# The state's part of the outputs as 64x64 matmuls, with r laid out by token half

## The chip, the cores and the metric

The kernel runs on one core of a Trainium2 chip. The metric is the device time of one execution in microseconds; the time before is the median of three runs. The engines are named as in the profile: PE (TensorE), ACT (ScalarE), DVE (VectorE), POOL (GpSimd), SP (the queue that issues most transfers).

## The reference

A linear attention with a decaying state (4 batches, 8 heads, 768 tokens, 48 values per head), followed by a dense two-layer network with SiLU on the 3072 tokens of 384 values:

```python
for t in range(S):
    cur = np.einsum('bhd,bhe->bhde', u[None] * kt, vt)
    y[:, :, t] = np.einsum('bhd,bhde->bhe', rt, state + cur)
    state = w[None, :, :, None] * state + np.einsum('bhd,bhe->bhde', kt, vt)
...
h = x @ w_in                       # 384 -> 2048
g = h * (1.0 / (1.0 + np.exp(-h)))
out = g @ w_out                    # 2048 -> 384
```

Inputs and outputs are float32.

## The kernel before

The tokens are cut into six chunks of 128, and a unit is one chunk of one batch: unit i is chunk i // 4 of batch i % 4, 24 units in all. Units are worked in pairs (i, i+1; the code calls the member e = 0 or 1). From unit 4 on a chunk is cut again into two halves of 64 tokens (x = 0 or 1). For the first half of a chunk the state that counts is the one carried from the chunk before; for the second half it is the state after the first half.

Heads lie in pairs: after `turn`, head 2p+j (j = 0 or 1) of r and k has its 48 values in partitions 64j to 64j+47 (rows 48 to 63 are a pad), with p and the token along the free dimension. `decay_one` multiplies by powers of w and gives `rT` and `kT` in float32; `cast_r` (L271) makes `rT16`, the 16-bit copy of `rT`, 112 partitions x 4 head pairs x 128 tokens.

The state stands in `st` in float32, 112 partitions: head j of each pair in rows 64j to 64j+47, 48 columns for each head pair p and member e. Two kinds of 16-bit copies of it feed the matmuls: `carry` (s0h in the profile, three buffers, the carried state) and `inner` (s1h, two buffers, the state after the first half). Before the change both are in a block form: for each member and head pair a matrix of 112 rows and 96 columns with head 0 in the upper left block, head 1 in the lower right one, and zeros elsewhere, set once at the start by five memsets (L143). `spread_state` (L330) writes the two blocks by two copies of 48 partitions x 384 elements. `first_state` does that on DVE for the first chunk, `state_first` on ACT for `inner`, `next_state` on POOL for `carry`.

The outputs of a pair, `outputs_halves` (L415), come in two groups of matmuls into two PSUM tiles `yp[e]`. The state's part (L424): for each head pair, member and half one matmul with 112 rows of `rT16` as weights (64 tokens) and the 96 columns of the block form, 16 matmuls. The attention's part (L433): for each head, member and half one matmul of 64 rows, 64 tokens and 48 columns, 32 matmuls. The half x and the member e set the rows of `yp` through `rows(e, x)`, so that the four matmuls of one head use four different quarters of the array.

PSUM has two tiles `att` for the transposes and the products of r and k, and four buffers under the tag `moe`, given out in turn to whatever asks: the network's first layer `hps`, its second layer `ops`, the sums `sp` and the outputs `yp`.

The order is written out by hand and each engine keeps it (`manual_schedule`). A list of words (`order`) places the steps of units 0 to 7 between pieces of the network (L and G for one tile of the first layer and its SiLU, H for both); in it `r16` is `cast_r` on ACT, `v16` the cast of v, `sd` the decay of the carried state, `sn` is `next_state`, `Z` the outputs and `z` their eviction. Then a loop runs over the pairs 6, 8, ..., 22. A round does: the sums of k and v (`sums`, L374), the products, both states, four network pieces (`fill(4)`), the outputs, the transposes of the next pair, the eviction on DVE, its transposed transfer, 4 pieces, the casts of v, then for each unit of the next pair two pieces and `cast_r` on DVE (L273), and 4 pieces more. A piece is one first-layer tile with its SiLU on ACT (L477, L485) or a quarter of a second-layer tile (L498), whose last quarter is followed by its copy `osb` (L504). When the pair is 2 or 3 of its chunk, sixteen first-layer and sixteen second-layer pieces are added to the list after the outputs.

Of the kernel before, what the change touches and what calls it, by code (L numbers as in the profile page):

```python
# [9 lines left out]
F16 = mybir.dt.float16  # L10
# [5 lines left out]
def kernel(  # L16
# [11 lines left out]
    nc = tc.nc  # L28

    B, H, S, D = r.shape  # L30
    C = 128
    NCH = S // C
    HD = H * D
    NP = H // 2
    PW = 2 * D
    PR = 64 + D
# [5 lines left out]
    HC = C // 2  # L42

    cst = ctx.enter_context(tc.tile_pool(name="cst", bufs=1))
    big = ctx.enter_context(tc.tile_pool(name="big", bufs=1))
    wrk = ctx.enter_context(tc.tile_pool(name="wrk", bufs=2))
# [3 lines left out]
    def unit(i):  # L50
        return divmod(i, B)
# [14 lines left out]
    st = [big.tile([PR, 2, NP, D], FP, name=f"st{b}") for b in range(B // 2)]  # L66
# [3 lines left out]
    def ld(i, dst, src, eng=nc.sync):  # L70
        sc, b = unit(i)
        eng.dma_start(
            out=dst[i % NIN][:, :, 0:D],
            in_=src[b, :, sc * C:sc * C + C, :].rearrange("h t d -> t h d"))
# [54 lines left out]
    for y in range(2):  # L129
# [5 lines left out]
        out=maskM, in_=maskM, compare_op=ALU.is_ge, fill=0.0,  # L135
# [1 line left out]
    ident16 = cst.tile([128, 128], F16)  # L137
    nc.gpsimd.tensor_copy(out=ident16, in_=ident)
    maskH = cst.tile([128, HC], FP)
    carry = [big.tile([PR, 2, NP, PW], F16, name=f"s0h{n}") for n in range(3)]  # L140
    inner = [big.tile([PR, 2, NP, PW], F16, name=f"s1h{n}") for n in range(2)]
    for t in carry + inner:
        nc.vector.memset(t, 0.0)  # L143
    for i in range(NIN):
        nc.gpsimd.memset(kc[i][:, :, D:64], 0.0)

# [62 lines left out]
    def L(i):  # L209
        return live.setdefault(i, {})  # L210
# [57 lines left out]
        decay_one(i, 0)  # L268
        decay_one(i, 1)

    def cast_r(i, copy=nc.vector.tensor_copy):  # L271
        L(i)["rT16"] = wrk.tile([PR, NP, C], F16, name="rT16", bufs=4)
        copy(out=L(i)["rT16"], in_=L(i)["rT"])  # L273

    def product_pair(i):
        a = [next_att().rearrange("p j (g c) -> p j g c", g=NP) for _ in range(2)]
# [50 lines left out]
    def carried_in(i):  # L327
        return carry[i // 2 % 3]

    def spread_state(copy, dst, src):  # L330
        for p0, c0 in ((0, 0), (64, D)):
            copy(out=dst[p0:p0 + D, :, :, c0:c0 + D], in_=src[p0:p0 + D])  # L332

    def first_state(i):
        _, b = unit(i)
        spread_state(nc.vector.tensor_copy, carried_in(i + B), L(i)["sps"])
        nc.vector.tensor_copy(out=st[b // 2], in_=L(i)["sps"])

    def rows(e, x):
        return HC * (x ^ e)  # L340

    def product_halves(i):
        a = next_att().rearrange("p j (e g c) -> p j e g c", e=2, g=NP)
        L(i)["a2"] = a
        for p in range(NP):
            for e in range(2):
                rT, kT = L(i + e)["rT"], L(i + e)["kT"]
                for x in range(2):
                    o0 = HC * x
                    for j, r0 in ((0, 0), (1, 64)):  # L350
                        nc.tensor.matmul(a[o0:o0 + HC, j, e, p, :],  # L351
                                         kT[r0:r0 + D, p, HC * x:HC * x + HC],
                                         rT[r0:r0 + D, p, HC * x:HC * x + HC],
                                         start=True, stop=True)
# [8 lines left out]
    def sums(i):  # L363
        sc, b = unit(i)
        xs = range(2 if sc < NCH - 1 else 1)
        L(i)["sp"] = [ps.tile([128, 512], FP, name="sp", tag="moe", bufs=4) for _ in xs]
        for p in range(NP):
            for e in range(2):
                for x in xs:
                    rows = slice(HC * x, HC * x + HC)  # L370
                    for j in range(2):
                        h = 2 * p + j
                        c0 = (e * NP + p) * D
                        nc.tensor.matmul(L(i)["sp"][x][64 * j:64 * j + 64, c0:c0 + D],  # L374
                                         kc[(i + e) % NIN][rows, h, :],
                                         L(i + e)["v16"][rows, h, :],
                                         start=True, stop=True)

    def flat(t):
        return t.rearrange("p e g n -> p (e g n)")  # L380

    def w_half():
        return wHT.unsqueeze(1).unsqueeze(3).broadcast_to([PR, 2, NP, D])

    def state_first(i):
        s1 = L(i)["s1"] = wrk.tile([PR, 2, NP, D], FP, name="s1")
        nc.vector.tensor_tensor(out=flat(s1), in0=L(i)["sp"][0][0:PR, 0:HD],  # L387
                                in1=flat(L(i)["sdec"]), op=ALU.add)
        spread_state(nc.scalar.copy, inner[i // 2 % 2], s1)

    def state_second(i):
        sc, b = unit(i)
        if sc == NCH - 1:
            return
        sd = wrk.tile([PR, 2, NP, D], FP, name="sd")
        nc.vector.tensor_tensor(out=sd, in0=L(i)["s1"], in1=w_half(), op=ALU.mult)
        nc.vector.tensor_tensor(out=flat(st[b // 2]), in0=L(i)["sp"][1][0:PR, 0:HD],
                                in1=flat(sd), op=ALU.add)

    def decayed_state(i):  # L400
        _, b = unit(i)
        L(i)["sdec"] = wrk.tile([PR, 2, NP, D], FP, name="sdec", bufs=3)
        nc.gpsimd.tensor_tensor(out=L(i)["sdec"], in0=st[b // 2], in1=w_half(), op=ALU.mult)

    def next_state(i):
        sc, b = unit(i)
        if sc == NCH - 1:
            return
        spread_state(nc.gpsimd.tensor_copy, carried_in(i + B), st[b // 2])
        decayed_state(i + B)  # L410

    def outputs_halves(i):
        yp = L(i)["y2"] = [ps.tile([128, 512], FP, name="yp", tag="moe", bufs=4)
                           for _ in range(2)]

        def place(e, x, c0, n):
            y0 = rows(e, x)
            return yp[e][y0:y0 + HC, c0:c0 + n]

        for p in range(NP):  # L420
            for e in range(2):
                for x in (e, 1 - e):
                    s = inner[i // 2 % 2] if x else carried_in(i)
                    nc.tensor.matmul(place(e, x, PW * p, PW),  # L424
                                     L(i + e)["rT16"][:, p, HC * x:HC * x + HC], s[:, e, p, :],
                                     start=(p == 0), stop=False, skip_group_check=True)
        for p in range(NP):
            for j in range(2):
                h = 2 * p + j
                for e in range(2):  # L430
                    for x in range(2):
                        r = HC * x
                        nc.tensor.matmul(place(e, x, D * h, D), L(i)["am2"][r:r + HC, j, e, p, :],  # L433
                                         L(i + e)["v16"][r:r + HC, h, :],
                                         start=False, stop=True, skip_group_check=True)

    def evict_halves(i):
        yp = L(i)["y2"]
# [117 lines left out]
    def piece(word, f):  # L556
# [12 lines left out]
        "vu": bonus_v,  # L569
        "Y": outputs_y, "y16": evict_first, "yT": turn_y, "xT": copy_x,  # L570
        "S": first_sums, "st": first_state, "ku": bonus_ku, "ru": bonus_rku, "rd": bonus_sum,
        "r16": lambda i: cast_r(i, nc.scalar.copy), "sd": decayed_state, "i_q": ld_win, "i_o": ld_wout,
        "Q": sums, "P": product_halves, "m": masked_halves, "s1_": state_first,
        "s2_": state_second, "sn": next_state, "Z": outputs_halves, "z": evict_halves,
        "lr": lambda i: ld(i, rin, r), "lk": lambda i: ld(i, kin, k), "lv": lambda i: ld(i, vin, v),
    }
    order = """
# [6 lines left out]
        L4.10 G4.10 T5 kT5 rT5 L4.11 G4.11 vu4 ru5 i_o0 v165 Q4 P4 s1_4 m4 rd5 s2_4 r165  # L584
        L4.12 G4.12 vu5 i_o1 L4.13 G4.13 Z4 z4 L4.14 G4.14 L4.15 G4.15 yT4 xT4
        yT5 xT5 T6 kT6 rT6 kc6 ku6 ru6 i_o2 H0 H1 v166 r166 H2 H3 T7 kT7 rT7 kc7 ku7 i_o3 v167
        r167 H4 ru7 rd6 sd6 vu6 sn4
    """
    for word in order.split():
        if "*" in word:  # L590
            n, word = word.split("*")
# [18 lines left out]
    for i in range(B + 2, NU, 2):  # L610
        sc, b = unit(i)
        nxt = range(i + 2, min(i + 4, NU))
        sums(i)
        product_halves(i)
        state_first(i)
        state_second(i)
        masked_halves(i)
        if i == B + 2:
            bonus_sum(i + 1)
            bonus_v(i + 1)  # L620
        for n in nxt:
            bonus_products(n)
            decayed_k(n)
        if i > B + 2 or sc < NCH - 1:
            next_state(i)
        fill(4)
        outputs_halves(i)
        for n in nxt:
            turn(n)
        evict_halves(i)  # L630
        turn_y_dma(i)
        turn_y_dma(i + 1)
        if b:
            fillers.extend((first(sc) if sc > 1 else rest_first(sc)) + second(sc))
        for n in nxt:
            decay(n)
        load(i + B)
        load(i + 1 + B)
        fill(4)
        for n in nxt:  # L640
            bonus_sum(n)
            cast_v(n)
            bonus_v(n)
        for n in nxt:
            fill(2)
            cast_r(n)
        fill(4)
    fill(len(fillers))

# [29 lines left out]
```

## Time and profile before

| what | value |
|---|---|
| median of 3 runs | 192.3 us (191.97 to 192.69) |
| the profiled execution's own time | 192.8 us |
| its span | 191.0 us |
| mean granted clock | 0.997 |
| PE busy | 180.1 us |
| ACT busy | 99.0 us |
| DVE busy | 114.7 us |
| POOL busy | 118.6 us |

The span is the time from the first to the last instruction of the profiled execution. A busy time is the union of an engine's instructions; matmuls are pipelined, so their rows overlap. In the timeline a row is the start in us, the time that the merged instructions took, engine, line, operation, output and inputs, shape, count, and in brackets the idle time before and what ended it. In the groups the columns are the count, the busy us, the mean ns of one, and the idle us before them with their causes. In the windows the columns are the stretch and its length, then the busy us and instructions of PE, PEld (weight loads), DVE, ACT and POOL, the granted clock, the share of the DMA engines and GB/s. The slices cut the span in 40 parts, with a digit for tenths busy.

### The profile page before, as it was taken

The page shows a single profiled execution, that of the slowest core. Times are in us where ns is not written, and L with a number is a line of the kernel's source. Part 1 is how long each engine was busy: PE and PEld are TensorE (multiplying, and loading weights), DVE is VectorE, ACT ScalarE, POOL GpSimd, SP SyncE. Part 2 cuts the span into 40 slices and gives each one's busy share as a digit, 9 for nine tenths or more (in the row PEclk, how much of TensorE's full clock was granted, in tenths as well). Part 3 has the DMA queues.
Part 4 walks back from the last instruction along what each step waited for, and adds up shares of the span by engine and source line. Part 5 has one row for each costly group of instructions (what it writes and reads, how often), then busy time and mean ns, then how long its engine had stood idle before and what let it go on. Part 6 is the DMA issues. An engine that isn't in the chain of part 4 may idle for free. (4 is left out here: it accounts for less than half of the span.)

```text
span 191.0 us, 6511 instructions
## 1 busy us (share of the span) xinstructions
PE 180.1 (94%) x2786; PEld 113.1 (59%) x2786; DVE 114.7 (60%) x189; ACT 99.0 (52%) x193; POOL 118.6 (62%) x151
## 2 busy tenths in 40 slices
PE   7798898998999999999999999999999999999993
PEld 2454783677666786655656655656646566444562
DVE  7578876845884794695686775766853944200120
ACT  5394477576433293158573178563267643289200
POOL 6499989699899977849649649749659130000000
PEclk9999999999999999999999999999999999999998
DMA  5999979999959469269177269177386202310022
GB/s 95 209 191 189 207 149 184 155 218 222 148 113 195 148 134 200 65 129 223 26 147 165 65 138 209 32 146 165 84 177 163 41 4 82 85 42 0 6 79 84
DMA packets 90272, 24.42 MB, mean 128 GB/s; under 512 B 83329, under 2 KB 90242, under 8 KB 90242
## 3 DMA queue, kind: packets, MB, share of 16 engines
q1 hardware_dynamic: 84992, 20.39, 49.1%
q0 software_dynamic: 3712, 3.15, 10.8%
q10 hardware_dynamic: 1538, 0.46, 1.1%
q8 instruction: 22, 0.36, 0.8%
q14 instruction: 8, 0.07, 0.1%
HBM read 20.65 MB, written 4.72 MB: 133 GB/s over the span
## 5 line engine op out<-in xcount | busy, mean ns | idle before, releaser
L477 PE MATMUL hps<-xT,win 128*128 128x512 f16 (+1 forms) x360 | 66.4, 337 | 1.0 <-DMA xT<-y 0.5
L485 ACT ACTIVATE gT<-hps 128x512 f16<-128x512 f32 x96 | 55.8, 597 | 17.4 <-PE hps L477 14.2
L498 PE MATMUL ops<-wout,gT 128*128 128x384 f16 x368 | 62.5, 326 | 0.0
L477 PEld LDWEIGHTS <-win 128*128 128x128 f16 x360 | 33.8, 98 | 26.8 <-issue 1.6
L498 PEld LDWEIGHTS <-gT 128*128 128x128 f16 x368 | 35.2, 98 | 23.4
L236 POOL TENSOR_TENSOR vu<-vin,rku 128x384 f32<-128x384 f32 x24 | 21.1, 892 | 21.0 <-DVE rku L231 21.0
L218 POOL TENSOR_TENSOR ku<-kin,u_bc 128x384 f32<-128x384 f32 x24 | 24.4, 1018 | 11.1 <-DMA kin<-in_k_dram 7.5
L504 ACT COPY osb<-ops 128x384 f32<-128x384 f32 x20 | 9.6, 479 | 41.7 <-PE ops L498 31.1
L305 DVE TENSOR_TENSOR y<-yp,vu 64x384 f16<-64x384 f32 (+1 forms) x34 | 18.9, 555 | 13.7 <-PE yp L433 5.0
L222 POOL TENSOR_TENSOR rku_f<-rin,ku 128x384 f32<-128x384 f32 x24 | 24.3, 1012 | 1.7
L226 POOL TENSOR_TENSOR kc<-kin,lamH 128x384 f16<-128x384 f32 x20 | 20.7, 1038 | 0.0
L259 DVE TENSOR_TENSOR kT<-att,lamK 112x512 f32<-112x512 f32 x24 | 16.4, 683 | 4.8 <-PE att L251 4.8
L387 DVE TENSOR_TENSOR s<-sp,sdec 112x384 f32<-112x384 f32 x10 | 5.6, 558 | 22.0 <-PE sp L374 20.7
L259 DVE TENSOR_TENSOR rT<-att,lamR 112x512 f32<-112x512 f32 x24 | 16.5, 686 | 2.5 <-PE att L251 1.1
L332 ACT CAST s1h<-s 48x384 f16<-48x384 f32 x20 | 10.2, 511 | 9.6 <-DVE s L387 9.5
L242 ACT CAST v<-vin 128x384 f16<-128x384 f32 x24 | 11.5, 511 | 5.4 <-DMA vin<-in_v_dram 5.2
L506 DVE COPY osb<-ops 128x384 f32<-128x384 f32 x3 | 1.7, 558 | 20.6 <-issue 16.5
L273 DVE CAST rT<-rT 112x512 f16<-112x512 f32 x16 | 13.9, 906 | 0.0
L231 DVE TENSOR_REDUCE rku<-rku_f 128x8 f32<-128x384 f32 x24 | 12.5, 544 | 1.4 <-POOL rku_f L222 1.4
L358 DVE TENSOR_TENSOR am<-att,maskH 128x1024 f16<-128x1024 f32 x10 | 12.2, 1218 | 1.2 <-PE att L351 1.2
L351 PE MATMUL att<-rT,kT 48*64 48x64 f32 x640 | 11.6, 220 | 0.0
L251 PE MATMUL att<-ident,kin 64*112 64x64 f32 x192 | 9.4, 217 | 1.5 <-DMA kin<-in_k_dram 1.5
(74 smaller groups left out, 167.1 us busy)
## 6 DMA issues: line engine op xcount, KB each, us to landing
rin<-in_r_dram SPq DMA_DIRECT2D x24, 192.0 KB, 3.7
vin<-in_v_dram SPq DMA_DIRECT2D x24, 192.0 KB, 4.3
kin<-in_k_dram SPq DMA_DIRECT2D x23, 192.0 KB, 4.5
out_dram<-osb SPq DMA_DIRECT2D x23, 192.0 KB, 2.7
win<-in_moe_w_in_dram POOLq DMA_DIRECT2D x4, 384.0 KB, 6.5
wout<-in_moe_w_out_dram POOLq DMA_DIRECT2D x4, 384.0 KB, 6.2
xT<-y SPq DMA_TRANSPOSE x18, 2.3
kin<-in_k_dram ACTq DMA_DIRECT2D x1, 192.0 KB, 3.7
```

Of the source, the lines that this page charges most:

```text
L218: nc.gpsimd.tensor_tensor(out=L(i)["ku"], in0=kin[i % NIN][:, :, 0:D], in1=u_bc, op=ALU.mult)
L222: nc.gpsimd.tensor_tensor(out=L(i)["rku_f"], in0=rin[i % NIN][:, :, 0:D], in1=L(i)["ku"], op=ALU.mult)
L226: nc.gpsimd.tensor_tensor(out=kc[i % NIN][:, :, 0:D], in0=kin[i % NIN][:, :, 0:D], in1=lamH if unit(i)[0] else lamC, op=ALU.mult)
L231: nc.vector.tensor_reduce(out=L(i)["rku"], in_=L(i)["rku_f"], axis=mybir.AxisListType.X, op=ALU.add)
L236: nc.gpsimd.tensor_tensor(out=L(i)["vu"], in0=vin[i % NIN], in1=L(i)["rku"].unsqueeze(2).broadcast_to([128, H, D]), op=ALU.mult)
L259: nc.vector.tensor_tensor(out=L(i)[key].rearrange("p g (y t) -> p y g t", y=2), in0=L(i)["t"][0:PR, :, x], in1=lam, op=ALU.mult)
L273: copy(out=L(i)["rT16"], in_=L(i)["rT"])
L305: nc.vector.tensor_tensor(out=y16[a], in0=y[b, 0:HD], in1=vu[a], op=ALU.add)
L358: nc.vector.tensor_tensor(out=am.rearrange("p j e g c -> p (j e g) c"), in0=L(i)["a2"].rearrange("p j e g c -> p (j e g) c"), in1=maskH.un ...
L477: nc.tensor.matmul(hps[:, f, :], win[:, q, (ft + f) * 128:(ft + f + 1) * 128], xts[sc][:, q, b0:b0 + nb, :].rearrange("p b t -> p (b t)"), ...
L485: nc.scalar.activation(out=gts[sc][:, ft:ft + m, b0 * C:(b0 + nb) * C], in_=hpss[b0, ft], func=AF.Silu)
L498: nc.tensor.matmul(opss[b], gts[sc][:, ft, b * C:(b + 1) * C], wout[:, ft, :], start=(ft == 0), stop=(ft == NFT - 1))
```

## The change

The block form goes. `carry` becomes 48 partitions x 2 members x 8 heads x 48, and `inner` the same in partitions 64 to 111; every head of the state then stands in the rows of one half of the tokens, and the five memsets go. The state's part of the outputs becomes 32 matmuls of 48 rows, 64 tokens and 48 columns, in the same order over heads, members and halves as the attention's.

For that r has to stand, for the first half of the tokens, in rows 0 to 47 for both heads of a pair, and for the second half in rows 64 to 111. Half of it already does; the other half is copied across by two copies of 48 partitions x 256 elements per unit into a new tile `rX16`. In the prelude ACT makes these copies, right after its cast. In the loop they are ACT's when the pair at hand is 2 or 3 of its chunk (b = 2), and DVE's otherwise; the cast stays on DVE. The copies of the state also cross partitions now. `next_state` keeps only the copy of head j = 0 on POOL, and that of j = 1 becomes a step of its own, `next_crossed`, on ACT, right after the outputs (`sx` in the written order, at its end for unit 4).

```diff
-    carry = [big.tile([PR, 2, NP, PW], F16, name=f"s0h{n}") for n in range(3)]
-    inner = [big.tile([PR, 2, NP, PW], F16, name=f"s1h{n}") for n in range(2)]
-    for t in carry + inner:
-        nc.vector.memset(t, 0.0)
+    carry = [big.tile([D, 2, H, D], F16, name=f"s0h{n}") for n in range(3)]
+    inner = [big.tile([PR, 2, H, D], F16, name=f"s1h{n}") for n in range(2)]
...
-    def cast_r(i, copy=nc.vector.tensor_copy):
-        L(i)["rT16"] = wrk.tile([PR, NP, C], F16, name="rT16", bufs=4)
-        copy(out=L(i)["rT16"], in_=L(i)["rT"])
+    def cast_r(i, copy=nc.scalar.copy, cross=nc.scalar.copy):
+        r16 = L(i)["rT16"] = wrk.tile([PR, NP, C], F16, name="rT16", bufs=4)
+        copy(out=r16, in_=L(i)["rT"])
+        rx = L(i)["rX16"] = wrk.tile([PR, NP, HC], F16, name="rX16", bufs=4)
+        for x in range(2):
+            cross(out=rx[64 * x:64 * x + D], in_=r16[64 - 64 * x:64 - 64 * x + D, :, HC * x:HC * x + HC])
+
+    def half_r(i, x, j):
+        rows = slice(64 * x, 64 * x + D)
+        return L(i)["rT16"][rows, :, HC * x:HC * x + HC] if j == x else L(i)["rX16"][rows]
...
-    def spread_state(copy, dst, src):
-        for p0, c0 in ((0, 0), (64, D)):
-            copy(out=dst[p0:p0 + D, :, :, c0:c0 + D], in_=src[p0:p0 + D])
+    def spread_state(copies, dst, src):
+        d0 = 64 if dst.shape[0] > D else 0
+        for j in range(2):
+            if copies[j]:
+                copies[j](out=dst[d0:d0 + D].rearrange("d e (g j) n -> d e g j n", j=2)[:, :, :, j, :],
+                          in_=src[64 * j:64 * j + D])
...
-        spread_state(nc.gpsimd.tensor_copy, carried_in(i + B), st[b // 2])
+        spread_state([nc.gpsimd.tensor_copy, None], carried_in(i + B), st[b // 2])
         decayed_state(i + B)
+
+    def next_crossed(i):
+        sc, b = unit(i)
+        if sc < NCH - 1:
+            spread_state([None, nc.scalar.copy], carried_in(i + B), st[b // 2])
...
-        for p in range(NP):
-            for e in range(2):
-                for x in (e, 1 - e):
-                    s = inner[i // 2 % 2] if x else carried_in(i)
-                    nc.tensor.matmul(place(e, x, PW * p, PW),
-                                     L(i + e)["rT16"][:, p, HC * x:HC * x + HC], s[:, e, p, :],
-                                     start=(p == 0), stop=False, skip_group_check=True)
...
+        quarters = [(e, x) for e in range(2) for x in range(2)]
+        for h in range(H):
+            p, j = divmod(h, 2)
+            for e, x in quarters:
+                s = inner[i // 2 % 2][64:64 + D] if x else carried_in(i)
+                nc.tensor.matmul(place(e, x, h), half_r(i + e, x, j)[:, p, :],
+                                 s[:, e, h, :], start=(h == 0), stop=False, skip_group_check=True)
...
         outputs_halves(i)
+        next_crossed(i)
         for n in nxt:
             turn(n)
...
-            cast_r(n)
+            cast_r(n, nc.vector.tensor_copy, nc.scalar.copy if b else nc.vector.tensor_copy)
```

More of the change, by code (lines that the diff above doesn't have):

```diff
@@ L328, in carried_in @@
         return carry[i // 2 % 3]
-    def spread_state(copy, dst, src):
-        for p0, c0 in ((0, 0), (64, D)):
-            copy(out=dst[p0:p0 + D, :, :, c0:c0 + D], in_=src[p0:p0 + D])
+    def spread_state(copies, dst, src):
[4 more added lines that the diff above has]
+                          in_=src[64 * j:64 * j + D])
     def first_state(i):
         _, b = unit(i)
-        spread_state(nc.vector.tensor_copy, carried_in(i + B), L(i)["sps"])
+        spread_state([nc.vector.tensor_copy] * 2, carried_in(i + B), L(i)["sps"])
         nc.vector.tensor_copy(out=st[b // 2], in_=L(i)["sps"])
@@ L388, in state_first @@
                                 in1=flat(L(i)["sdec"]), op=ALU.add)
-        spread_state(nc.scalar.copy, inner[i // 2 % 2], s1)
+        spread_state([nc.scalar.copy] * 2, inner[i // 2 % 2], s1)
     def state_second(i):
@@ L414, in outputs_halves, with place @@
                            for _ in range(2)]
-        def place(e, x, c0, n):
+        def place(e, x, h):
             y0 = rows(e, x)
-            return yp[e][y0:y0 + HC, c0:c0 + n]
-        for p in range(NP):
-            for e in range(2):
-                for x in (e, 1 - e):
-                    s = inner[i // 2 % 2] if x else carried_in(i)
-                    nc.tensor.matmul(place(e, x, PW * p, PW),
-                                     L(i + e)["rT16"][:, p, HC * x:HC * x + HC], s[:, e, p, :],
-                                     start=(p == 0), stop=False, skip_group_check=True)
[L427 to L435, printed above, removed]
+            return yp[e][y0:y0 + HC, D * h:D * h + D]
+        quarters = [(e, x) for e in range(2) for x in range(2)]
[5 more added lines that the diff above has]
+                                 s[:, e, h, :], start=(h == 0), stop=False, skip_group_check=True)
+        for h in range(H):
+            p, j = divmod(h, 2)
+            for e, x in quarters:
+                r = HC * x
+                nc.tensor.matmul(place(e, x, h), L(i)["am2"][r:r + HC, j, e, p, :],
+                                 L(i + e)["v16"][r:r + HC, h, :],
+                                 start=False, stop=True, skip_group_check=True)
     def evict_halves(i):
@@ L571 @@
         "S": first_sums, "st": first_state, "ku": bonus_ku, "ru": bonus_rku, "rd": bonus_sum,
-        "r16": lambda i: cast_r(i, nc.scalar.copy), "sd": decayed_state, "i_q": ld_win, "i_o": ld_wout,
+        "r16": cast_r, "sd": decayed_state, "i_q": ld_win, "i_o": ld_wout,
         "Q": sums, "P": product_halves, "m": masked_halves, "s1_": state_first,
-        "s2_": state_second, "sn": next_state, "Z": outputs_halves, "z": evict_halves,
+        "s2_": state_second, "sn": next_state, "sx": next_crossed, "Z": outputs_halves, "z": evict_halves,
         "lr": lambda i: ld(i, rin, r), "lk": lambda i: ld(i, kin, k), "lv": lambda i: ld(i, vin, v),
@@ L586 @@
         yT5 xT5 T6 kT6 rT6 kc6 ku6 ru6 i_o2 H0 H1 v166 r166 H2 H3 T7 kT7 rT7 kc7 ku7 i_o3 v167
-        r167 H4 ru7 rd6 sd6 vu6 sn4
+        r167 H4 ru7 rd6 sd6 vu6 sn4 sx4
     """
```

## The prediction

> **What bounds the kernel now.** I read the page first: its engine totals and slices.
>
> ```profile
> PE 180.1 (94%) x2786; PEld 113.1 (59%) x2786; DVE 114.7 (60%) x189; ACT 99.0 (52%) x193; POOL 118.6 (62%) x151
> ...
> PE   7798898998999999999999999999999999999993
> ...
> ACT  5394477576433293158573178563267643289200
> ...
> PEclk9999999999999999999999999999999999999998
> ```
>
> TensorE is the bound, at full granted clock; ScalarE (ACT) is half idle on average. The windows view says since when:
>
> ```profile
> 40.00:60.00 20.00, 18.81 (x306) 13.41 (x305) 12.79 (x21) 9.82 (x20) 18.94 (x23) 1.00 0.99 176
> 60.00:80.00 20.00, 20.00 (x451) 15.24 (x451) 14.31 (x21) 8.86 (x17) 17.63 (x22) 1.00 0.59 145
> 80.00:100.00 20.00, 20.00 (x264) 11.25 (x263) 15.25 (x25) 13.06 (x24) 12.13 (x15) 1.00 0.60 128
> ```
>
> From about 52 us to 160 PE (the first value after the length) never rests. There matmuls start at their shortest spacing (0.65 us per three of 512 columns), one loop round takes 13.81 us, and nothing else costs time. So in the loop a shorter PE step is gained in full, and a new PE wait lost in full. Before 52 us PE waits for ACT and for loads. Next, one outputs step in the PE timeline:
>
> ```profile
> 91.68 0.23 PE L424 MATMUL yp<-s0h,rT 112*64 112x96 f16 x1
> ...
> 92.14 0.44 PE L433 MATMUL yp<-v,am 64*64 64x48 f16 x32
> 92.51 0.27 PE L251 MATMUL att<-ident,rin 64*112 64x64 f32 x2
> ```
>
> The state's 16 matmuls hold PE from 91.68 to 92.14, 0.46 us, 0.13 of that between the last one's start (92.00) and the attention's first. The attention's 32 take 0.37 to the next step. Their 0.44 less one duration (0.19, tile view) is 0.25 from first start to last: eight groups of four, 0.032 a group.
>
> **The change on PE.** The state becomes 32 matmuls of exactly the attention's shape in the same four quarters of the array, and the attention follows with no change of shape. Eight more groups at 0.032 are 0.25 us, in place of 0.46: 0.21 saved per outputs step. Eight of the ten steps (64 to 161 us) lie in the saturated stretch: 8 x 0.21 = 1.7 us gained. The steps at 36 and 49 us are counted below.
>
> The Trainium skill speaks against this in "TensorEngine Tiling (Array Packing)", Restrictions and Gotchas: different row tiles cannot access one PSUM bank at once, and each pair of quarters here shares a bank. The attention's rows contradict it: four matmuls, two of one bank, start within 0.011 us. By the page's rule the total below would be some 2 us higher (an estimate from that page).
>
> **What ACT gets.** ScalarE receives, per unit in the prelude (4 units) and in the rounds whose pair is 2 or 3, two crossing copies of 48x256; and once per round a 48x384 state copy (taken from POOL). Prices, from the groups view:
>
> ```profile
> L242 ACT CAST v<-vin 128x384 f16<-128x384 f32 x24 | 11.5, 511 | 5.4 <-DMA vin<-in_v_dram 5.2
> L332 ACT CAST s1h<-s 48x384 f16<-48x384 f32 x20 | 10.2, 511 | 9.6 <-DVE s L387 9.5
> L273 ACT CAST rT<-rT 112x512 f16<-112x512 f32 x4 | 2.5, 618 | 0.3 <-DVE rT L259 0.3
> L159 ACT CAST rin<-idle 128x128 f32<-128x128 f16 x4 | 1.2, 296 | 0.0
> ```
>
> 128, 384 and 512 elements per partition take 0.296, 0.511 and 0.618: about 0.19 plus 0.83 ns an element, whatever the types. 256 elements: 0.40 us. Bounds: 0.30 (128 elements) and 0.51 (384). The two s1h rows of a pair, on different partitions, follow each other with a gap of 0.01 and no overlap; a pair of crossings also changes partitions, so it is 0.82. Whole-height rows behind schedule do overlap: silus start 0.49 apart (97.80, 98.29) and last 0.59, a 0.10 overlap that stays a rival for the crossings.
>
> The skill's "ScalarE: Activation LUTs", What ACT_TABLE_LOAD costs, has back-to-back activations overlap by about 0.093 us, with no exception named. The silus agree, the s1h pair does not. With that rule each stall below would be near 0.6 and the total about 193 (an estimate from that page).
>
> *State copy in the loop.* It comes after the outputs, where ACT is idle from 92.38 to 94.41; 0.51 fits. Cost nothing; without that cover it would be 0.51 a round.
>
> *Crossings in the loop (rounds 10, 14, 18).* ACT is first in, first out, and behind the crossings queue the silus that free PSUM. The timelines of ACT, PE and DVE at round 14:
>
> ```profile
> 112.17 0.48 ACT L504 COPY osb<-ops 128x384 f32<-128x384 f32 x1 [1.17 <-issue]
> 112.77 3.19 ACT L485 ACTIVATE gT<-hps 128x512 f16<-128x512 f32 x5
> 116.40 1.04 ACT L332 CAST s1h<-s 48x384 f16<-48x384 f32 x2 [0.44 <-DVE s L387]
> ```
> ```profile
> 111.92 3.40 PE L477 MATMUL hps<-xT,win 128*128 128x512 f16 x15
> 115.25 0.22 PE L374 MATMUL sp<-v,kc 64*64 64x48 f16 x4
> ```
> ```profile
> 111.56 1.78 DVE L273 CAST rT<-rT 112x512 f16<-112x512 f32 x2
> 115.81 0.56 DVE L387 TENSOR_TENSOR s<-sp,sdec 112x384 f32<-112x384 f32 x1 [2.46 <-PE sp L374]
> ```
>
> PE makes five tiles a to e, then the two sp tiles. "moe" has four buffers in turn, so sp's first tile takes b's and its second c's: the sums wait for the silus of b and c. Now these end at 114.02 and 114.66, 1.2 and 0.59 us early. After the change ACT's order is two crossings, osb, silu a, two crossings, silus b to e. The casts (0.82 and 1.05) end at 112.38 and 113.34. Laid out: crossings 112.41 to 113.23; osb 113.25 to 113.73; a 113.64 to 114.23; crossings 114.25 to 115.07; b to 115.69; c to 116.18. With 0.05 for the semaphore the second sp tile may begin at 116.23, not 115.25: PE stands 0.98 us. The bounds 0.30 and 0.51 give 0.6 and 1.4. Then the backlog is gone: s1h follows silu e (to 117.15), and the next silu waits for PE. Rounds 10 and 18 have the same offsets. Cost 3 x 0.98 = 2.9 us. Round 6 crosses too, but between L2 tiles of 2.6 us each: its osb copies end at 58.7 and 60.1, before anyone waits.
>
> *Prelude.* Here ACT already holds PE back:
>
> ```profile
> 33.26 0.41 PE L374 MATMUL sp<-v,kc 64*64 64x48 f16 x28 [0.94 <-ACT v L242]
> ...
> 36.60 0.20 PE L424 MATMUL yp<-s1h,rT 112*64 112x96 f16 x1 [0.40 <-ACT gT L485]
> ```
>
> Unit 4's crossings (30.06 to 30.88) push the silus, but ACT had 0.71 idle before the one at 32.21, so v16 of unit 5 ends 0.17 late. Unit 5's stand between r16 and the silus: silu 12 ends at 37.68, not 36.55, and PE's outputs resume at 37.74, not 36.60; with 0.21 saved there PE is 0.9 behind. With that 0.9, ACT's next row is r16 of unit 6 43.62 to 44.24, crossings to 45.09, two silus to 46.20, and v16 of unit 7 ends at 46.60, not 44.71: the sums of units 6 and 7 wait for it, and PE is 1.9 behind. Part returns, as the next wait of PE (0.46 at 46.90, for DVE's s, held by POOL's sdec until 46.72) disappears. Unit 7's r16 and crossings (to 47.97), a silu (48.59), the carry copy (49.12), s1h (50.17) and two silus (51.28) let the outputs go on at 51.33 and finish at 51.91, not 50.33. PE's wait for a load there (kin, to 51.67) disappears too. PE starts its second layer at 52.95 in place of 52.04: 0.9 us lost (laid out with the two other copy prices: 0.5 and 1.3).
>
> **The rest.** Five memsets (L143, 1.98 us) go from DVE's start. Their cover stays: the first products wait for kin's landing (PE idle until 5.81, then 0.70 until 8.28), so no gain. In rounds 8, 12, 16, 20 DVE makes four crossings. No row shows a 16-bit SBUF copy there; between the 0.17 of a small memset and the 1.05 of a whole cast I take 0.45, half a cast for half the elements: 1.8 us into an idle 2.46 that ends with L387. Nothing, unless one takes over 0.7 (the 2.46, and 0.5 that s1h may be late). POOL loses a 0.5 us copy per round, off the path; SP's queue keeps its sequence. The other spread copies keep their size.
>
> **Sum.** Span 191.0 + 0.9 - 1.7 + 2.9 = 193.1; 1.8 us lie around the profiled span (192.8 in all), so 194.9. The median of the runs, 192.3, lies 0.5 below that execution: 194.4.
>
> **Rivals.**
> 1. *Faster:* ACT hides the crossings. Only the PE gain is left, 1.7 plus some 0.2 in the prelude: 190.4. The place is the sums of rounds 10, 14, 18; no stall needs a crossing of 0.15 us or less, break-even of the whole some 0.25. For: ACT is 52% busy. Against: the fixed part alone is 0.19. Chance 0.09.
> 2. *The copies overlap* by the 0.10 of the silus: four copies stand ahead of silu c, so stalls of 0.58, prelude 0.6: 192.3 - 1.7 + 1.7 + 0.6 = 192.9. The gaps of the s1h pair are against it. 0.12.
> 3. *The state's quarters go two at a time, not four:* sixteen groups, 0.51 us, so 0.05 lost per step where I gain 0.21: 8 x 0.26 = 2.1 above the forecast, 196.5. The attention's rows are against it. 0.05.
> 4. *DVE's crossings overrun:* at 1.05 each, 4.2 - 2.96 = 1.2 us in each of four rounds, 5.0: 199.4. 0.03.
>
> The forecast holds 0.71; its two copy prices give 192.3 + 0.5 - 1.7 + 1.8 = 192.9 and 192.3 + 1.3 - 1.7 + 4.2 = 196.1. From 192.6 to 196.2 I take in these and rival 2, and leave out the other three and the tails. 0.5% (0.96 us, about what a measurement of this kernel can tell from no change) puts the borders at 191.3 and 193.3. Faster 0.08, same 0.14, slower 0.78.
>
> **What would show it.** In the changed profile: the state and attention 64 matmuls in 0.62 us; crossings near 0.40 on ACT in pairs of 0.82; PE idle near 1 us before the second sp tile, released by silu, in three rounds and in no others; PE's second layer starting near 53. A PE with no wait at the sums proves me wrong; so do crossings under 0.25, or a state block over 0.4.

## The result, and the profile after

The changed kernel takes 195.0 us (median of 6 runs, 194.5 to 195.94), the kernel before beside it 192.57. The ratio is 1.0126, 95% interval 1.0088 to 1.0164: slower by 1.3%. One of the six executions of the kernel before, at 195.51, was in a slower state and is left out of the ratio. The profiled execution took 194.5 us, with a span of 192.8.

The page of the changed kernel, totals and slices:

```profile
PE 178.8 (93%) x2946; PEld 112.5 (58%) x2946; DVE 122.0 (63%) x200; ACT 110.4 (57%) x225; POOL 114.3 (59%) x143
...
PE   7798897798999999998999998999999999999993
...
ACT  5394478779723784159693169673269563189200
```

PE has 160 matmuls more and is busy 1.3 us less, yet the span is longer: what was full from slice 11 on now has slices of 8. Its timeline at the outputs of round 12:

```profile
93.47 0.21 PE L438 MATMUL yp<-s0h,rT 48*64 48x48 f16 x1
...
93.74 0.42 PE L444 MATMUL yp<-v,am 64*64 64x48 f16 x32
94.10 0.27 PE L249 MATMUL att<-ident,rin 64*112 64x64 f32 x2
```

The state's part runs from 93.47 to 93.74, 0.27 us where it held PE 0.46, and both parts 0.63 where they held 0.83. The same round's sums, PE first, then ACT ahead of them:

```profile
87.71 0.81 PE L488 MATMUL hps<-xT,win 128*128 128x512 f16 x3
88.95 0.21 PE L382 MATMUL sp<-v,kc 64*64 64x48 f16 x2 [0.43 <-ACT gT L496]
89.44 0.34 PE L382 MATMUL sp<-v,kc 64*64 64x48 f16 x19 [0.28 <-ACT gT L496]
```
```profile
85.62 0.82 ACT L274 COPY rX<-rT 48x256 f16<-48x256 f16 x2 [1.42 <-DVE rT L271]
86.46 0.48 ACT L515 COPY osb<-ops 128x384 f32<-128x384 f32 x1
86.84 0.60 ACT L496 ACTIVATE gT<-hps 128x512 f16<-128x512 f32 x1
87.47 0.82 ACT L274 COPY rX<-rT 48x256 f16<-48x256 f16 x2
88.31 2.06 ACT L496 ACTIVATE gT<-hps 128x512 f16<-128x512 f32 x4
```

The order laid out in the prediction is there, row by row: pair of crossings, osb, silu a, pair of crossings, silus b to e. PE stops twice, once for each sp tile. The bracketed idle (0.43 and 0.28) is less than the time lost, since the last tile's rows overlap the stop; the lost time is read from starts, below.

To see where time goes I compare the start of the same PE step in two traces. The table gives the delay in us against the kernel before: at the products of units 2 and 3 (start, 17.94 us before), then at the outputs of each round.

| kernel | start | 8 | 10 | 12 | 14 | 16 | 18 | 20 | 22 |
|---|---|---|---|---|---|---|---|---|---|
| before, at us | 17.94 | 64.00 | 77.87 | 91.68 | 105.49 | 119.30 | 133.12 | 146.90 | 160.69 |
| the change | -0.34 | 0.64 | 1.03 | 1.79 | 1.59 | 2.48 | 2.28 | 2.57 | 2.37 |
| e1_loop_cross_dve | -0.15 | 3.22 | 6.72 | 6.51 | 6.31 | 6.11 | 5.90 | 5.70 | 5.50 |
| e2_no_cross | 0.40 | 0.07 | 0.95 | 0.76 | 0.56 | 0.37 | 0.17 | -0.03 | -0.24 |
| e3_before_with_cross | 0.23 | 0.94 | 0.94 | 1.90 | 1.90 | 2.86 | 2.86 | 3.35 | 3.35 |
| e4_state_copy_pool | -0.40 | 0.09 | -0.09 | 0.70 | 0.52 | 1.31 | 1.14 | 1.43 | 1.23 |
| e7_loop_dve_pool_copies | 0.44 | 0.93 | 1.88 | 1.70 | 1.52 | 1.35 | 1.17 | 0.97 | 0.76 |
| e8_round6_act | 0.82 | 1.80 | 2.23 | 2.02 | 1.82 | 1.62 | 1.42 | 1.21 | 1.01 |
| e9_swap_halves | 0.79 | 1.64 | 1.43 | 2.20 | 2.00 | 2.76 | 2.58 | 2.88 | 2.68 |
| e10_prelude_alone | 0.16 | 0.31 | 0.84 | 1.60 | 1.39 | 2.15 | 2.08 | 2.38 | 2.18 |
| e6_prelude_order | 1.12 | 0.70 | 0.86 | 0.69 | 0.60 | 0.42 | 0.24 | 0.04 | -0.16 |

Where the delay falls by 0.2 from one column to the next, an outputs step was gained and nothing lost. A stall at the sums of 0.96 shows as a rise of 0.76, since a gain of 0.2 falls between the same two columns.

### The profile page after: what moved, and what is told of

It reads as the page before. It is cut to its first block, busy times and chain, and to the rows that moved or that the text cites. A ratio compares the mean times of both kernels' runs of the same rounds, so it can differ in the third digit from the quotient of the medians.

```text
span 192.8 us, 6867 instructions
## 1 busy us (share of the span) xinstructions
PE 178.8 (93%) x2946; PEld 112.5 (58%) x2946; DVE 122.0 (63%) x200; ACT 110.4 (57%) x225; POOL 114.3 (59%) x143
## 4 chain that ended last, share of the span: by engine, by line
POOL 48%; PE 23%; issue 20%; DMA 2%; DVE 2%; ACT 2%; ACTq 0%; POOLq 0%
POOL ku L216 12%; POOL rku_f L220 10%; PE ops L509 10%; PE hps L488 9%; POOL kc L224 9%; POOL vu L234 9%; POOL sdec L411 3%; DMA u_bc<-in_u_dram 2%; POOL s0h L339 2%; PE ops L534 1%; POOL win L83 1%; POOL wout L88 1%; PE att L359 1%; DVE rT L257 1%; ACT rX L274 1%
## 5 line engine op out<-in xcount | busy, mean ns | idle before, releaser
L496 ACT ACTIVATE gT<-hps 128x512 f16<-128x512 f32 x96 | 54.5, 598 | 14.5 <-PE hps L488 12.2
L216 POOL TENSOR_TENSOR ku<-kin,u_bc 128x384 f32<-128x384 f32 x24 | 25.3, 1056 | 11.4 <-DMA kin<-in_k_dram 8.2
L271 DVE CAST rT<-rT 112x512 f16<-112x512 f32 x16 | 15.0, 958 | 0.1
L274 ACT COPY rX<-rT 48x256 f16<-48x256 f16 x24 | 9.7, 403 | 9.4 <-DVE rT L271 9.0
```

Of the source, the lines that this page charges most:

```text
L216: nc.gpsimd.tensor_tensor(out=L(i)["ku"], in0=kin[i % NIN][:, :, 0:D], in1=u_bc, op=ALU.mult)
L271: copy(out=r16, in_=L(i)["rT"])
L496: nc.scalar.activation(out=gts[sc][:, ft:ft + m, b0 * C:(b0 + nb) * C], in_=hpss[b0, ft], func=AF.Silu)
```

## The experiments

**Undoing one side: the crossings of the loop on DVE.**

```diff
-            cast_r(n, nc.vector.tensor_copy, nc.scalar.copy if b else nc.vector.tensor_copy)
+            cast_r(n, nc.vector.tensor_copy, nc.vector.tensor_copy)
```

> All crossing copies of the loop on DVE; the prelude as in the change. Theory A (ACT's crossings in rounds 10, 14, 18 hold back the silus, and the sums of the next rounds wait for PSUM: 0.97 + 0.96 + 0.47 = 2.4 us in the profile of the change): PE's idle before the sp tiles of the next rounds is gone, and the span falls by 2.4 us from 192.8 to about 190.4 (time near 192.3, ratio to before 0.998), as long as DVE's four crossings per round fit in its 2.46 us idle before L395. Theory B (the loss sits in the state copies or in the sheer amount of ACT work): it stays within 0.5 us of 195.0. Theory C (DVE cannot take them, its 16-bit copies wait for POOL): L395 is late, PE waits at the outputs for am or s1h instead, 193 to 195.

199.67 us, ratio 1.0348 (1.0284 to 1.0413). From round 10 on it does what theory A says: -0.2 in every step, no stall. But 5.9 us are lost between the sums of round 8, where the delay is 0.83, and the outputs of round 10: theory C in kind, far larger than its 193 to 195, and from one round alone. The traced execution, 197.71, was the fastest of its runs; it accounts for 5.0 of the 7.5 us, and no trace shows the rest. DVE in round 6:

```profile
57.84 0.74 DVE L271 CAST rT<-rT 112x512 f16<-112x512 f32 x1
58.61 4.80 DVE L274 COPY rX<-rT 48x256 f16<-48x256 f16 x2
63.43 1.14 DVE L271 CAST rT<-rT 112x512 f16<-112x512 f32 x1
64.61 1.97 DVE L274 COPY rX<-rT 48x256 f16<-48x256 f16 x2
66.61 0.56 DVE L395 TENSOR_TENSOR s<-sp,sdec 112x384 f32<-112x384 f32 x1
```

A pair of crossings that takes 0.44 at its best took 4.80, and `s`, the state after the first half, which the sums of round 8 feed, came 6.2 late.

**The PE side alone: no crossings.**

```diff
-        rx = L(i)["rX16"] = wrk.tile([PR, NP, HC], F16, name="rX16", bufs=4)
-        for x in range(2):
-            cross(out=rx[64 * x:64 * x + D], in_=r16[64 - 64 * x:64 - 64 * x + D, :, HC * x:HC * x + HC])
+        L(i)["rX16"] = rx_fixed
```

> Crossing copies left out everywhere: the crossed half of r is a tile of zeros set once at the start, so the outputs lack that part of the state; all else as in the change. Theory A: the PE gain of 0.21 us per outputs step shows in full in the eight saturated steps (1.7 us), no silu is late in the loop, and the prelude keeps only the state copy's 0.5: time 190.3 to 191.0, ratio 0.989 to 0.993. Theory B (the smaller matmuls do not pay, or the state copies on ACT cost): 192 or more.

192.05 us, ratio 0.9989 (0.9968 to 1.0011): 1.0 above theory A and inside theory B. The table splits it. From round 10 to 22 the delay falls by 1.19 in six steps, 0.2 each, without one stall, as forecast. The start is 0.40 late, and round 8 loses 0.88 net, with its own gain of 0.2 taken off: the second DVE cast of round 6 took 4.04 us here too, with no crossing in the kernel. So theory B's first reason, that the smaller matmuls do not pay, is out; its second, that the moved state copy costs, holds in part. The long cast comes with the state copy, not with the crossings.

**The cost side alone: the kernel before with the crossings added.**

```diff
-            cast_r(n)
+            cast_r(n, nc.vector.tensor_copy, nc.scalar.copy if b else nc.vector.tensor_copy)
```

(with `cast_r` as in the change, in the prelude too)

> The kernel before, with the crossing copies of the change added at the same places on the same engines (their tile is written and never read); block form, matmuls and state copies as before. Theory A: the crossings alone make the loss, prelude 0.9 + stalls 2.4 (0.97, 0.96, 0.47): time 195.4 to 196.0, ratio 1.016. Theory B (the loss belongs to the matmuls or the state copies): within 0.6 us of 192.5.

196.58 us, ratio 1.0207 (1.0158 to 1.0255). The loop adds 0.96, 0.96 and 0.49 in rounds 12, 16, 20 and nothing elsewhere; the prelude adds 0.71. This is theory A in kind, with a time 0.6 above its range; of the 3.6 us that the traced span is longer, these four make 3.1, and a later start (0.23) and a longer wait at the end the rest. The block form with its long matmuls stalls in the same way:

```profile
89.07 0.21 PE L377 MATMUL sp<-v,kc 64*64 64x48 f16 x2 [0.42 <-ACT gT L488]
89.56 0.43 PE L377 MATMUL sp<-v,kc 64*64 64x48 f16 x30 [0.28 <-ACT gT L488]
```

**The state copy back on POOL.**

```diff
-        spread_state([nc.gpsimd.tensor_copy, None], carried_in(i + B), st[b // 2])
+        spread_state([nc.gpsimd.tensor_copy] * 2, carried_in(i + B), st[b // 2])
```

(and `next_crossed` does nothing)

> Both halves of the carried state copied by POOL again, as before; the crossings and matmuls as in the change. Theory A: in the loop ACT's state copy lay in an idle of ACT, so its return brings nothing there; in the prelude s1h of units 6 and 7 comes 0.5 earlier, for some 0.3 of PE: 194.5 to 194.8. On the cast of round 6 that took 4.04 us on DVE in the change (0.72 before) while POOL worked without a pause from 58.7 to 62.1 us: if it waits for a pause of POOL, the second copy on POOL brings the pause back, the cast is under 1.1 us, and the wait of PE in round 8 (0.6) goes too: near 194.0. If it has another cause it stays at about 4 us. Theory B (the state copy on ACT is the loss): 192.5 to 193.

194.16 us, ratio 1.0096 (1.0062 to 1.0130), near the 194.0 of theory A. The stalls stay, the second cast of round 6 takes 0.72, and round 8 gains its 0.2 instead of losing 0.4. The prelude loses 0.49 (from -0.40 to 0.09) where the change loses 0.98, more than the 0.3 expected.

**One edit for the stalls: rounds 10, 14, 18 on DVE, round 6 still on ACT.**

```diff
-            cast_r(n, nc.vector.tensor_copy, nc.scalar.copy if b else nc.vector.tensor_copy)
+            cast_r(n, nc.vector.tensor_copy, nc.scalar.copy if i == B + 2 else nc.vector.tensor_copy)
```

> The change with one edit: the crossings of rounds 10, 14 and 18 on DVE in place of ACT; round 6 and the prelude stay on ACT, the state copy stays split between POOL and ACT. Theory A: the idle of PE at the sums of rounds 12, 16, 20 (0.97, 0.96, 0.47) is gone and nothing else moves, the 4 us cast of round 6 stays: span 192.8 less 2.4, 190.4, time 192.1, ratio to before 0.998 to 1.000. Rival (the loop loss is in the state copies on ACT or in DVE): 194 or more.

193.08 us, ratio 1.0029 (0.9995 to 1.0063), 1.0 above the forecast, though the stalls are gone and every step from round 10 gains 0.2. This execution had started 1.16 later than the change's (0.82 against -0.34), which its span of 191.3 contains; between the start and round 22 it loses 0.19, the change 2.71. The other runs have no trace, so whether late starts explain the whole miss is open. DVE takes four crossings a round from round 8 on, and PE does not wait for them.

**What holds DVE's cast: the same POOL work, other partitions.**

```diff
-        spread_state([nc.gpsimd.tensor_copy, None], carried_in(i + B), st[b // 2])
+        spread_state([None, nc.gpsimd.tensor_copy], carried_in(i + B), st[b // 2])
```

(ACT takes head j = 0)

> The change with the two halves of the carried state swapped: POOL copies head j = 1 (from partitions 64 to 111), ACT head j = 0. POOL does the same number of instructions as in the change. In the kernel before POOL paused 0.06 us before and 0.08 us after its copy from these partitions, and not around the other one. Theory A (DVE's cast of round 6 gets in at a pause of POOL): the pauses come back with this copy, and the second cast takes under 1.1 us, not 4.04; PE's wait in round 8 is under 0.1 us. Rival (the number or the time of POOL's instructions decides): the cast stays at about 4 us.

Theory A's numbers came true. One execution, 194.77 us, with a start 1.13 later than the change's. The timelines of DVE and POOL in round 6, the change first:

```profile
57.64 4.70 DVE L271 CAST rT<-rT 112x512 f16<-112x512 f32 x2
```
```profile
58.03 0.70 POOL L339 CAST s0h<-st 48x384 f16<-48x384 f32 x1
58.70 0.82 POOL L411 TENSOR_TENSOR sdec<-st,wHT 112x384 f32<-112x384 f32 x1
59.48 1.61 POOL L234 TENSOR_TENSOR vu<-vin,rku 128x384 f32<-128x384 f32 x2
61.05 1.00 POOL L216 TENSOR_TENSOR ku<-kin,u_bc 128x384 f32<-128x384 f32 x1
62.13 1.07 POOL L220 TENSOR_TENSOR rku_f<-rin,ku 128x384 f32<-128x384 f32 x1
```

and with the halves swapped:

```profile
58.12 1.38 DVE L271 CAST rT<-rT 112x512 f16<-112x512 f32 x2
```
```profile
57.58 1.00 POOL L224 TENSOR_TENSOR kc<-kin,lamH 128x384 f16<-128x384 f32 x1
58.64 0.58 POOL L339 CAST s0h<-st 48x384 f16<-48x384 f32 x1
59.30 0.89 POOL L411 TENSOR_TENSOR sdec<-st,wHT 112x384 f32<-112x384 f32 x1
60.15 1.61 POOL L234 TENSOR_TENSOR vu<-vin,rku 128x384 f32<-128x384 f32 x2
```

In the change each POOL row starts as the one before ends or a little earlier, until the 0.08 between 62.05 and 62.13; DVE's second cast begins at 58.30 and ends at 62.34. Swapped, POOL's copy leaves 0.06 before it and 0.08 after it (58.58 to 58.64, 59.22 to 59.30), the cast takes 0.72, and PE has no wait in round 8. The profile calls its spans on POOL rough, so the pauses are read only because they recur: around this copy they are 0.06 and 0.08 in every trace that has it on POOL.

The first cast of the round needs no pause. In the change it ends in 0.74 although POOL's kc and s0h overlap by 0.06, and so do first casts of later rounds, here beside two vu rows that overlap by 0.04 (85.31 and 85.26):

```profile
57.64 0.74 DVE L271 CAST rT<-rT 112x512 f16<-112x512 f32 x1
```
```profile
84.77 0.82 DVE L271 CAST rT<-rT 112x512 f16<-112x512 f32 x1
```
```profile
84.48 1.80 POOL L234 TENSOR_TENSOR vu<-vin,rku 128x384 f32<-128x384 f32 x2 [3.66 <-DVE rku L229]
```

So the swap shows which copy on POOL the short cast goes with, and that the number of POOL's rows is not the reason. That the pause itself is the reason is not shown.

**All of the loop on DVE, with POOL's copies.**

```diff
-            cast_r(n, nc.vector.tensor_copy, nc.scalar.copy if b else nc.vector.tensor_copy)
+            cast_r(n, nc.vector.tensor_copy, nc.vector.tensor_copy)
...
+        spread_state([nc.gpsimd.tensor_copy] * 2, carried_in(i + B), st[b // 2])
```

(and `next_crossed` does nothing)

> All crossings of the loop on DVE, and both halves of the carried state copied by POOL. Theory A (a DVE copy from SBUF to SBUF finishes only when POOL pauses; POOL pauses twice in round 6, after each of its copies, and then not until 62 us): two or three of the six DVE copies of round 6 get through, the rest wait until 62, L395 of round 8 is 2 to 5 us late instead of 6.2, and the time is 194 to 198. Rival (the copies only share bandwidth with POOL, and run at up to 1.05 us each): six copies take at most 6 us from 56.8, L395 is late by 2.4 at most and PE by under 2: 191.5 to 193.

192.86 us in one execution: the rival's number, not theory A's, although `s` came 2.7 late, beyond the rival's 2.4 and within theory A's 2 to 5. DVE in round 6:

```profile
58.43 0.97 DVE L274 COPY rX<-rT 48x256 f16<-48x256 f16 x2
59.41 1.16 DVE L271 CAST rT<-rT 112x512 f16<-112x512 f32 x1
60.60 2.48 DVE L274 COPY rX<-rT 48x256 f16<-48x256 f16 x2
```

Two crossings got through at POOL's two pauses, but the cast (to 60.57) and the crossing after it (to 61.34) ended where POOL's rows show none; only the last crossing (1.74) waited for a pause. So theory A's "only when POOL pauses" is wrong as a rule; what lets a DVE copy through between two POOL rows was not found.

**Better versions.** First with the crossings on ACT only in the prelude and round 6, and POOL's copies:

```diff
-            cast_r(n, nc.vector.tensor_copy, nc.scalar.copy if b else nc.vector.tensor_copy)
+            cast_r(n, nc.vector.tensor_copy, nc.scalar.copy if i == B + 2 else nc.vector.tensor_copy)
...
+        spread_state([nc.gpsimd.tensor_copy] * 2, carried_in(i + B), st[b // 2])
```

(and `next_crossed` does nothing)

> Crossings on ACT in the prelude and in round 6 only, on DVE in all later rounds; both halves of the carried state copied by POOL. Theory A (2.4 us of stalls come from ACT's crossings in rounds 10, 14, 18; the long cast of round 6 from POOL not pausing, cured by its second copy): the span is that of the run with POOL's copies, 191.9, less 2.4: 189.5, time about 191.2, ratio 0.993. If DVE's crossings are held up in later rounds too, 192 to 194.

192.1 us, ratio 0.9977 (0.9948 to 1.0006): no measurable change, and the 0.993 forecast lies below the interval. Its trace is not in the table. Then also the prelude's order:

```diff
-        L4.10 G4.10 T5 kT5 rT5 L4.11 G4.11 vu4 ru5 i_o0 v165 Q4 P4 s1_4 m4 rd5 s2_4 r165
+        L4.10 G4.10 T5 kT5 rT5 L4.11 G4.11 vu4 ru5 i_o0 v165 r165 Q4 P4 s1_4 m4 rd5 s2_4
...
-        yT5 xT5 T6 kT6 rT6 kc6 ku6 ru6 i_o2 H0 H1 v166 r166 H2 H3 T7 kT7 rT7 kc7 ku7 i_o3 v167
-        r167 H4 ru7 rd6 sd6 vu6 sn4 sx4
+        yT5 xT5 T6 kT6 rT6 kc6 ku6 ru6 i_o2 H0 H1 v166 H2 H3 T7 kT7 rT7 kc7 ku7 i_o3 v167
+        r166 r167 H4 ru7 rd6 sd6 vu6 sn4 sx4
```

> As the kernel with crossings on ACT only in the prelude and round 6 and POOL's copies, and in the prelude r16 and crossing of unit 5 stand before s1 of unit 4 (where ACT waited 1.16 us for DVE), those of unit 6 behind the cast of v of unit 7. Theory A: PE's waits at 36 us (1.4) and before the sums of units 6 and 7 (0.95 in all) shrink to those of the kernel before (0.4 and 0.2), a further 0.3 to 0.7 us: span about 189.0, time 190.5 to 190.9, ratio 0.990. Rival (the prelude's PE waits are made good by the later waits for sdec and kin anyway): same as without the reordering, 191.2.

191.3 us, ratio 0.9931 (0.9901 to 0.9961): faster than both kernels, 0.4 above what was forecast. Round 8 still loses 0.36 in its trace (0.70 to 0.86, with 0.20 gained): DVE's sd (L404), the decay of the state, takes 1.76 beside POOL's rows, 1.22 in the kernel before. The outputs of unit 4, where PE stopped 1.38 us in the change, go on after 0.2:

```profile
37.25 0.21 PE L438 MATMUL yp<-s0h,rT 48*64 48x48 f16 x1
37.25 0.21 PE L438 MATMUL yp<-s1h,rX 48*64 48x48 f16 x1
37.47 0.18 PE L438 MATMUL yp<-s0h,rT 48*64 48x48 f16 x1
```

**The prelude's order alone, on the change.** (the same edit of the order)

> The change with the prelude's order alone changed: r16 and crossings of unit 5 before s1 of unit 4, those of unit 6 behind the cast of v of unit 7. Theory A: the delay that PE gathers between its first product and the sums of round 8 falls from 0.98 us against the kernel before to about -0.4, as in the run with this order; the stalls at the sums of rounds 12, 16 and 20 stay at 0.97, 0.96 and 0.47. Rival (this needs POOL's copies too): over 0.5 stays.

194.26 us in one execution. The prelude's cost falls from 0.98 to 0.15 (0.16 at the start, 0.31 at round 8), not to -0.4; the three stalls stay (0.97, 0.96, 0.50, as sums of the table's steps and the 0.2). So the order alone is worth 0.83, and the rival is right about the rest. A late start is not what makes e6's prelude cheaper: with the state copy split the old order loses 0.98 both from -0.34 (the change) and from 0.82 (e8), and with POOL's copies 0.49 both from -0.40 (e4) and from 0.44 (e7). POOL's copies are worth 0.49 in the old order and 0.57 in the new one (0.15 against -0.42), about the 0.51 of the copy that they take from ACT.

## Why the prediction was right

The time fell within the range and on the forecast side: 194.4 was forecast, 195.0 measured beside a before of 192.57, so +2.4 in place of +2.1. In the span of the two profiled executions it is +1.8: the one before lay 0.5 above its median (192.8 and 192.3), the one after 0.5 below (194.5 and 195.0), and the steps account for these two alone. By its steps, from the table and the starts between its columns:

| step | forecast | measured |
|---|---|---|
| outputs in the loop | -1.7 | 8 x 0.20 = -1.6 |
| stalls at the sums | 2.9 | 0.97 + 0.96 + 0.49 = 2.4 |
| prelude | 0.9 | 0.98 (-0.34 to 0.64) |
| wait in round 8 | none | 0.60 |
| wait in round 14 | none | 0.13 |
| start | none | -0.34 |
| last transposed transfer | none | -0.42 |
| sum | 2.1 | 1.75 |

That the sum came so near is partly luck: a wait of 0.60 that was not foreseen stands against a third stall 0.5 too large in the forecast and 0.76 at the start and the end that do not belong to the change.

*The PE gain* held to 0.01 us a step. The columns from 10 to 22 of e2 and of e1 show it without anything else. Rival 3 (two quarters at a time) is out: 0.27 for the state's block. The attention's rows had been the right price, and the rule on row tiles and PSUM banks in "TensorEngine Tiling (Array Packing)" of the Trainium skill does not hold in these rows either: four matmuls, two of one bank, from different rows of the array, start within 0.01 us.

*The stalls* were right in place, cause and size for two of three: 0.97 where 0.98 was laid out. The third was mis-sized. "Rounds 10 and 18 have the same offsets" is true of ACT, but round 20 belongs to the last chunk, whose sums have one sp tile; it waits for silu b alone, 0.49. Rival 1 needed a crossing of 0.15 us or less and rival 2 an overlap. The groups of the changed kernel have neither:

```profile
L271 DVE CAST rT<-rT 112x512 f16<-112x512 f32 x16 | 15.0, 958 | 0.1
L274 ACT COPY rX<-rT 48x256 f16<-48x256 f16 x24 | 9.7, 403 | 9.4 <-DVE rT L271 9.0
L274 DVE COPY rX<-rT 48x256 f16<-48x256 f16 x16 | 7.1, 445 | 0.4
```

0.403 each on ACT, and 0.82 a pair with a gap of 0.01. The overlap that "ScalarE: Activation LUTs" gives for back-to-back activations is absent between the two copies of a pair, which are on different partitions.

*The prelude* came as laid out: 0.98 for 0.9. The outputs of unit 4 stop for 1.38 us, behind the crossings of unit 5, where they had stopped for 0.40:

```profile
33.06 0.41 PE L382 MATMUL sp<-v,kc 64*64 64x48 f16 x28 [1.08 <-ACT v L240]
...
37.36 0.18 PE L438 MATMUL yp<-s0h,rT 48*64 48x48 f16 x1 [1.38 <-ACT gT L496]
```

Half of the 0.98 is not the crossings but the carry copy, which the prediction had laid out on ACT too: with that copy back on POOL the same order loses 0.49 (e4, e7).

*The step that failed* is "POOL loses a 0.5 us copy per round, off the path". POOL's own time was off the path, but the copy taken from it had two pauses around it, at which DVE's second cast of round 6 came through. Without that copy the cast took 4.04 us, `s` and am (the masked products, which the attention's part of the outputs reads) came late, and round 8 lost 0.60. In e4 and e9 that copy is back on POOL and the wait is gone; e9 has the same number of POOL rows as the change, so their number is not the reason. Whether the pause is, or something else about that copy, stays open. The Trainium skill states under "SBUF — State Buffer", Who interferes with whom, that DVE in a 2-port mode, which casts and copies can enter, and GpSimd share a port pair under an exclusive lock, and that whoever issues first blocks the other for a whole instruction. The cast at 84.77, which ends 0.28 after the vu row beside which it began, agrees with that. That a cast is held off over five POOL rows, as in round 6, is beyond the page. The 0.45 taken for a DVE crossing was the mean (0.445), but of unlike prices: 0.22 alone, 0.73 to 1.06 beside POOL. Rival 4 ("overrun") did not come true in the rounds that it named; e1 made it true in round 6.

*Round 14* lost 0.13 at am: DVE's sd took 1.43 there, 0.77 before, with POOL working beside it in both. *Start and end* are no effect of the change as far as these runs show: the start lay between -0.40 and 1.12 in the tabled runs, with and without the five memsets (0.23 with them, -0.40 without). At the end PE no longer waits 0.48 for the last transposed transfer; SP issued the one before it in 1.43 us, not 1.87; in the other runs that wait was between nothing and 0.67.

## What to carry to other kernels

In a kernel whose TensorE is full, price a change by laying out, buffer by buffer, who frees the next matmul's PSUM tile: ACT was 52% busy on average, and four copies of 0.4 us among the silus of a round still cost a microsecond in two rounds of three. Look also at how the engines off the path stand beside each other: one copy taken from POOL made a DVE cast wait 4 us, and PE 0.6. The gain was real, and it could be had by putting the copies where the queue had room: crossings on DVE in the rounds full of silus, and the prelude's copies in ACT's wait for DVE, for a ratio of 0.9931.

## What the runs showed of the hardware

- A DVE cast from SBUF to SBUF can wait for POOL. Usually the wait is for one row: the cast at 84.77 in the change took 0.82 and ended 0.28 us after the vu row beside which it began, with no pause before the next one. In round 6 of the change, e2, e8 and e10 the second cast took 4.04 to 4.05 us, over five POOL rows that followed each other without a pause, and ended 0.28 to 0.29 us after the next pause began; with pauses of 0.06 and 0.08 us it took 0.72. What decides between the two is not shown.
- In the rows of round 6 POOL paused 0.06 before and 0.08 us after a copy that reads partitions 64 to 111, and not around one of partitions 0 to 47.
- ACT's crossing pairs have a gap of 0.01, where whole-height rows behind schedule overlap by 0.1. But a copy of 48 partitions can overlap too: in the loop of the change ACT's s0h copy, which reads partitions 64 to 111, began 0.10 to 0.11 us before the row ahead of it ended; in e9, where it reads 0 to 47, it began 0.02 behind it.
- Alone, a 48x256 16-bit copy took 0.22 us on DVE and 0.40 on ACT; the 112x512 cast took 0.43 on DVE between two such copies, and 0.72 to 1.16 beside POOL where it did not take 4 us.
